# Two loads of q back in SyncE's queue, and the last output product split 384 to 128 columns

## The chip, the cores and the metric

The kernel runs on one core of one Trainium2 chip. The metric is the device time of the whole program in microseconds (us), of which several runs are taken; lower is better. A profiled execution gives the times inside: the span from the first to the last instruction, and the start and length of each instruction and DMA packet. A core has five engines that run side by side and meet at semaphores: TensorE (PE; its weight loads stand apart as PEld), VectorE (DVE), ScalarE (ACT), GpSimd (POOL) and SyncE (SP). DMAs are issued by SyncE, ScalarE or GpSimd, each in a queue of its own (q1, q10 and q0 in the profile), and all are carried by the same 16 DMA engines.

## The reference

A decaying linear attention over 4 batches, 8 heads, 768 tokens and 64 columns a head, in blocks of 64 tokens, and then a gated block with a product across tokens:

```python
for b in range(nb):                       # blocks of 64 tokens
    intra = einsum('bhic,bhjc->bhij', qb, kb) * Dmask
    intra = einsum('bhij,bhjd->bhid', intra, vb)
    inter = einsum('bhid,bhde->bhie', qb * lam_pow, kv_state)
    out[:, :, sl] = intra + inter
    kv_state = lam_block * kv_state + einsum('bhsd,bhse->bhde', kb * rev_pow, vb)
x = out.transpose(0, 2, 1, 3).reshape(B, S, 512)
h = maximum(x @ w_in, 0)                  # 512 -> 1024
u, v = h[..., :512], h[..., 512:]
v_n = (v - mean(v)) / sqrt(var(v) + 1e-6)
v_s = einsum('ts,bsd->btd', w_spatial, v_n) + b_spatial
result = (u * v_s) @ w_out                # 512 -> 512
```

Inputs and result are fp32.

## The kernel before

The 4 x 768 tokens are cut into 12 steps of 256 tokens, three to a batch (`n` from 0 to 11). A step loads 256 tokens of k, q and v for all heads, 512 KB each (`LK`, `LQ`, `LV`, in `load`, L191; three buffers for each input), casts them to bf16 (`KC`, `QC`; L174 to L178), multiplies v by powers of lam (`VD`, L314), turns k and q (by TensorE: `TK`, `TQ`, L328; from step 7 on by a DMA), computes scores (`SC`, L369) and masks them (`MK`, L373), adds to the state (`KV`, L385; copied out by `SS`), forms the attention output (`AV`, L406 and L415; copied out by `EX`), and multiplies by the two halves of w_in (`PV`, L438, and `PU`, L485). The v half is normalised (`BN`, `RA`, `RD`, `VN`). When a batch's three steps are done, its product across tokens (`PW`, L506), bias (`GB`, L511), gate (`GM`, L517) and output product (`PO`, L522, for each of 6 tiles of 128 tokens) follow, woven among the next steps; `EO` copies a tile's output from PSUM to SBUF and `ST` stores it (L545).

The order of all this is written by hand: `ORDER` is a list of tokens, each an operation, its arguments and, as the last letter, the engine that issues it (T, D, A, P, S for TensorE, VectorE, ScalarE, GpSimd, SyncE). `LQ.1.2.A` is the load of q of step 1, whole, issued by ScalarE; `LQ.1.2.S` the same by SyncE. Each engine takes its own tokens in the order of the list; tokens of other engines between them mean nothing to it. Waits between engines follow from the data and the buffers.

SyncE issues the loads in the order k0, k1, v0, v1, k2, q2, v2, q3, k3, ... ScalarE issues lam, then q0 and q1. GpSimd issues the weights: two halves of w_in (`WI`, L257), two of w_spatial (`WS`, L262), later w_out. It has these tokens in this order (casts and products of its own among them): k0's cast, `GT.0.1` (a one-element copy named "seen", L253, which waits until k of step 1 has landed), `WI.0`, q1's cast, `VD.1.0`, `WI.1`, `VD.1.1`, k2's cast, `WS.1`, `GT.2.1` (the same for v of step 1), `WS.0`, `VD.2.0`, `VD.2.1`. So the weights' transfers start when loads of k, v and k have come in and GpSimd has got that far.

TensorE begins with products on a constant tile (`WU`, L212), then takes q0 and k0, k1, the scores of step 0, the state, q1 and so on; `TQ.2.6` (q of step 2) comes after the first `PV`s, and `KV.2.0` after two `PU`s.

The last tile of the last batch (`t` = 4) is done in two halves of 256 columns: `PH` (L528) multiplies a half, `EH` copies it out (the first by ScalarE, the second by VectorE), `SH` stores it (the first in ScalarE's queue, the second in SyncE's; L541).

Of the kernel before, what the change touches and what calls it, by code (L numbers as in the profile page):

```python
# [13 lines left out]


ORDER = """
LK.0.2.S lam.A LQ.0.2.A LQ.1.2.A pos.P LK.1.2.S LV.0.2.S idn.P WU.-8.T LB.1.T msk.P LN.1.A LL.D LX.A KC.0.2.P
LT.0.A LV.1.2.S QC.0.2.D mkc.A WU.29.T TQ.0.6.T LK.2.2.S TK.0.1.T GT.0.1.P WI.0.P KC.1.2.D EK.0.1.A EQ.0.6.D
WU.5.T TK.1.4.T LQ.2.2.S LT.1.A SC.0.1.5.T SC.0.0.1.T VD.0.0.D VD.0.1.D LV.2.2.S LT.2.A MK.0.0.1.D WU.7.T
KV.0.0.T QC.1.2.P MK.0.1.5.D EK.1.4.A WU.8.T TQ.1.2.T LQ.3.2.S SS.0.0.A AV.0.0.0.T EQ.1.2.D VD.1.0.P SY.0.0.A  # L20
# [63 lines left out]
def kernel(  # L84
# [13 lines left out]
    P = 128  # L98
    B, H, S, D = q.shape
    DM = H * D  # L100
# [68 lines left out]
    def bank(b, n=1):  # L169
        return ps[:, b] if n == 1 else ps[:, b:b + n]  # L170

    def copy(e, o, i):
        if e == "A":
            nc.scalar.activation(out=o, in_=i, func=AF.Copy)  # L174
        elif e == "D":
            nc.vector.tensor_copy(out=o, in_=i)  # L176
        else:
            nc.gpsimd.tensor_copy(out=o, in_=i)  # L178
# [344 lines left out]
                             rhs=wout_sb[:, f, :], start=(f == 0), stop=(f == NCH - 1))  # L523

    def p_h(e, bb, t, b, x):
        half = slice(x * (DM // 2), (x + 1) * (DM // 2))
        for f in range(NCH):
            nc.tensor.matmul(out=bank(b)[:, half], lhsT=gT[bb % 2][:, f, t * P:(t + 1) * P],  # L528
                             rhs=wout_sb[:, f, half], start=(f == 0), stop=(f == NCH - 1))
# [2 lines left out]
        copy(e, o_sb[:, (bb * NT + t) % NO], bank(b))  # L532

    def e_h(e, bb, t, b, x):
        half = slice(x * (DM // 2), (x + 1) * (DM // 2))
        copy(e, o_sb[:, (bb * NT + t) % NO, half], bank(b)[:, half])

    def s_h(e, bb, t, x):
        half = slice(x * (DM // 2), (x + 1) * (DM // 2))
        eng = {"S": nc.sync, "A": nc.scalar}[e]  # L540
        eng.dma_start(out=out[bb, t * P:(t + 1) * P, half], in_=o_sb[:, (bb * NT + t) % NO, half])  # L541

    def st_o(e, bb, t):
# [4 lines left out]
               LK=ld_k, LQ=ld_q, LV=ld_v, KC=k_c, QM=q_m, DK=d_k, DQ=d_q, QC=q_c, VD=v_d, TK=t_k, TQ=t_q, EK=e_k, EQ=e_q,  # L548
               SC=s_c, MK=m_k, KV=k_v, SS=s_s, AV=a_v, SY=s_y, EX=e_x, PV=p_v, EV=e_v, BN=b_n, RA=r_a, RD=r_d,
               VN=v_n, PU=p_u, EU=e_u, WT=w_t, EW=e_w, PW=p_w, GB=g_b, GM=g_m, PO=p_o, EO=e_o, ST=st_o, EH=e_h, SH=s_h, PH=p_h)  # L550
    with tc.manual_schedule():
        for token in ORDER.split():
# [32 lines left out]
```

## Time and profile before

| | |
|---|---|
| time, median of 3 runs | 156.41 us (155.68 to 156.83) |
| the profiled execution's own time | 155.68 us |
| its span | 154.0 us |
| mean granted TensorE clock | 0.989 |
| TensorE busy | 137.1 us (89%) |
| VectorE, ScalarE, GpSimd busy | 106.1, 89.9, 69.8 us |
| SyncE's queue q1 | 27.01 MB, 68.6% of 16 engines' span |
| GpSimd's queue q0 | 2.75 MB, 10.3% |
| ScalarE's queue q10 | 1.18 MB, 3.0% |
| loads of q by ScalarE, of k by SyncE | 8.1 and 7.1 us from issue to landing (median) |

A share is a mean over stages that have different limits. The chain that ended last is followed back from the last instruction: at each step to what released it. It goes through TensorE for 68% of the span, DVE 10%, waits for DMAs 9%, SyncE's issues 6%. A wait is put down to the releaser that came last by the profile; where that one shares no data with the waiting instruction, it was another. Times below are counted from the span's start.

### The profile page before, as it was taken

To read this page: it belongs to the slowest core of one execution; us is meant where nothing else is said; L and a number is where in the kernel's file an instruction comes from. 1 tells how busy PE (TensorE), PEld (TensorE's weight loads), DVE (VectorE), ACT (ScalarE), POOL (GpSimd) and SP (SyncE) were. 2 spreads that over 40 slices of the span, in tenths; PEclk is the share of its full clock that TensorE was granted. 3 is DMA by queue.
4 is the path that set the end of the run, shared out by engine and by line. 5 is a ranking of instruction groups with operands and counts; after the bars stand their busy time and mean duration, and the time that the engine had idled before them with its cause. 6 is when DMAs were issued, how large, how long until landed. Compare 5 with 4: busy or idle time off the path is not lost.

```text
span 154.0 us, 4860 instructions
## 1 busy us (share of the span) xinstructions
PE 137.1 (89%) x2060; PEld 90.5 (59%) x2075; DVE 106.1 (69%) x191; ACT 89.9 (58%) x167; POOL 69.8 (45%) x83
## 2 busy tenths in 40 slices
PE   6967774969999999839999999999999999999990
PEld 4746542456876786635565657655676756565540
DVE  1247724688999679989976778885469888748300
ACT  3968373566850677417799824678373647960270
POOL 7435650055008999827255564564644002014700
PEclk9999998799999999999999999999999999999999
DMA  3999999999999969965999997999797000052364
GB/s 91 300 290 289 237 241 235 220 281 257 281 285 285 257 169 280 235 165 105 231 282 172 245 233 184 320 201 288 164 292 172 2 6 0 0 198 79 136 231 178
DMA packets 54152, 31.25 MB, mean 203 GB/s; under 512 B 11634, under 2 KB 51058, under 8 KB 54130
## 3 DMA queue, kind: packets, MB, share of 16 engines
q1 hardware_dynamic: 49520, 27.01, 68.6%
q0 software_dynamic: 2384, 2.75, 10.3%
q10 hardware_dynamic: 2226, 1.18, 3.0%
q8 instruction: 16, 0.26, 0.7%
q14 instruction: 6, 0.05, 0.1%
HBM read 24.77 MB, written 6.29 MB: 202 GB/s over the span
## 4 chain that ended last, share of the span: by engine, by line
PE 68%; DVE 10%; DMA 9%; SPq 6%; ACT 2%; issue 2%; POOL 1%; DVEq 0%
PE ps L506 19%; PE ps L522 13%; PE ps L438 11%; PE ps L485 10%; DMA q_in<-in_q_dram 9%; SPq L191 6%; DVE gT L517 3%; PE ps L369 3%; PE ps L415 3%; DVE a_sb L373 2%; PE ps L328 2%; PE ps L385 2%; PE ps L406 2%; PE ps L498 1%; POOL vd L314 1%
## 5 line engine op out<-in xcount | busy, mean ns | idle before, releaser
L517 POOL TENSOR_TENSOR gT<-vsb,uT 128x384 bf16<-128x384 f32 x24 | 21.8, 917 | 40.1 <-DVE vsb L511 31.4
L506 PE MATMUL ps<-wt_sb,vn 128*128 128x384 bf16 x192 | 33.9, 326 | 0.0
L373 DVE TENSOR_TENSOR a_sb<-ps,m 128x1024 bf16<-128x1024 f32 x24 | 28.6, 1216 | 2.2 <-PE ps L369 1.9
L314 POOL TENSOR_TENSOR vd<-v_in,lv 128x512 bf16<-128x512 f32 x19 | 19.6, 1043 | 18.5 <-DVE a_sb L373 10.7
L506 PEld LDWEIGHTS <-vn 128*128 128x128 bf16 x192 | 18.3, 98 | 11.9
L485 PE MATMUL ps<-xT,win_sb 128*128 128x256 bf16 x192 | 24.4, 273 | 0.0
L438 PE MATMUL ps<-win_sb,xT 128*128 128x512 bf16 x87 | 23.6, 400 | 0.4
L511 DVE TENSOR_TENSOR vsb<-ps,bsp 128x384 f32<-128x384 f32 x32 | 17.2, 550 | 9.5 <-PE ps L506 9.5
L522 PE MATMUL ps<-wout_sb,gT 128*128 128x512 bf16 x86 | 21.4, 379 | 0.4 <-issue 0.2
L443 ACT ACTIVATE vh<-ps 128x512 bf16<-128x512 f32 x23 | 13.7, 596 | 13.4 <-PE ps L438 12.4
L485 PEld LDWEIGHTS <-win_sb 128*128 128x128 bf16 x192 | 18.4, 98 | 4.9
L174 ACT ACTIVATE o_sb<-ps 128x512 f32<-128x512 f32 (+1 forms) x23 | 13.1, 586 | 11.3 <-PE ps L522 11.3
L174 ACT ACTIVATE xT<-ps 128x512 bf16<-128x512 f32 x22 | 15.2, 742 | 6.6 <-PE ps L415 6.4
L453 DVE BATCH_NORM_STATS2 st<-vh 128x6 f32<-128x512 bf16 x24 | 16.3, 679 | 2.7 <-ACT vh L443 2.6
L438 PEld LDWEIGHTS <-xT 128*128 128x128 bf16 x96 | 9.2, 102 | 10.4 <-issue 1.7
L385 PE MATMUL ps<-vd,kc 64*64 64x64 bf16 x320 | 8.9, 193 | 6.2 <-DVE s_sb L176 2.9
L522 PEld LDWEIGHTS <-gT 128*128 128x128 bf16 x92 | 8.8, 98 | 9.3 <-issue 0.2
L443 ACT ACTIVATE uT<-ps 128x512 bf16<-128x512 f32 x20 | 11.7, 596 | 2.8 <-PE ps L485 2.4
L299 POOL TENSOR_TENSOR qc<-q_in,lqn 128x512 bf16<-128x512 f32 x10 | 10.7, 1071 | 5.1 <-DMA q_in<-in_q_dram 4.7
L385 PEld LDWEIGHTS <-kc 64*64 64x64 bf16 x320 | 7.4, 109 | 8.3 <-issue 7.3
L174 ACT ACTIVATE s_sb<-ps 128x256 bf16<-128x256 f32 x16 | 6.1, 382 | 8.3 <-PE ps L385 7.4
L415 PE MATMUL ps<-a_sb,vd 64*64 64x128 bf16 x384 | 10.5, 217 | 0.3 <-DVE a_sb L373 0.3
(72 smaller groups left out, 179.7 us busy)
## 6 DMA issues: line engine op xcount, KB each, us to landing
k_in<-in_k_dram SPq DMA_DIRECT2D x12, 512.0 KB, 7.1
v_in<-in_v_dram SPq DMA_DIRECT2D x12, 512.0 KB, 6.9
out_dram<-o_sb SPq DMA_DIRECT2D x23, 256.0 KB, 3.1
q_in<-in_q_dram SPq DMA_DIRECT2D x10, 512.0 KB, 7.8
wsp_raw<-in_moe_w_spatial_dram POOLq DMA_DIRECT2D x2, 576.0 KB, 11.0
q_in<-in_q_dram ACTq DMA_DIRECT2D x2, 512.0 KB, 8.1
win_sb<-in_moe_w_in_dram POOLq DMA_DIRECT2D x2, 512.0 KB, 9.7
wout_sb<-in_moe_w_out_dram POOLq DMA_DIRECT2D x1, 512.0 KB, 9.3
```

Source lines behind the costliest of these rows:

```text
L174: nc.scalar.activation(out=o, in_=i, func=AF.Copy)
L314: vec(e).tensor_tensor(out=vd[n % NCA].rearrange("p (o i w) m d -> p o i (w m) d", o=2, i=2)[o], in0=v_in[n % NIN].rearrange("p (o i w) m ...
L373: nc.vector.tensor_tensor(out=a_sb[n % NA][:, i].rearrange("p o w j x -> p (o w) (j x)"), in0=bank(b, 2).rearrange("p o (w y) -> p (o w) y ...
L385: nc.tensor.matmul(out=pkv[row(o), u], lhsT=kc[n % NCA][row(c), u, m, o, :], rhs=vd[n % NCA][row(c), 4 * o + u, m, :], start=new and u == ...
L438: nc.tensor.matmul(out=bank(b), lhsT=x[:, g % 2, c, c ^ (g // 2)], rhs=win_sb[:, g, DH:DFF], start=(g == 0), stop=(g == NCH - 1))
L443: nc.scalar.activation(out=o, in_=i, func=AF.Relu)
L453: nc.vector.bn_stats(out=st6[p2][:, t], in_=vh[p2][:, t])
L485: nc.tensor.matmul(out=pu[:, f2].rearrange("p (c x) -> p c x", c=2), lhsT=win_sb[:, g, f * P:(f + 1) * P], rhs=x[:, 4 * i + o:4 * i + 4 - ...
L506: nc.tensor.matmul(out=bank(b)[:, 0:HW], lhsT=vn[bb % 2][:, s, f * P:(f + 1) * P], rhs=wt_sb[:, s, i * HW:(i + 1) * HW], start=(s == 0), s ...
L511: nc.vector.tensor_tensor(out=vsb[(bb * 4 + f) % NVS][:, i * HW:(i + 1) * HW], in0=bank(b)[:, 0:HW], in1=bsp[:, i * HW:(i + 1) * HW], op=A ...
L517: vec(e).tensor_tensor(out=gT[bb % 2][:, f, cols], in0=vsb[(bb * 4 + f) % NVS][:, cols], in1=uT[bb % 2][:, f, cols], op=ALU.mult)
L522: nc.tensor.matmul(out=bank(b), lhsT=gT[bb % 2][:, f, t * P:(t + 1) * P], rhs=wout_sb[:, f, :], start=(f == 0), stop=(f == NCH - 1))
```

## The change

It has two parts. The loads of q of steps 0 and 1 are issued by SyncE and no longer by ScalarE: that of step 0 after k of step 0, that of step 1 after v of step 0, so that SyncE's queue has k0, q0, k1, v0, q1, v1, k2, q2, v2, ... And the two parts of the last tile's output product, of its copies and of its stores are 384 and 128 columns wide in place of 256 and 256. Nothing else differs.

```diff
 ORDER = """
-LK.0.2.S lam.A LQ.0.2.A LQ.1.2.A pos.P LK.1.2.S LV.0.2.S idn.P WU.-8.T LB.1.T msk.P LN.1.A LL.D LX.A KC.0.2.P
+LK.0.2.S lam.A pos.P LQ.0.2.S LK.1.2.S LV.0.2.S idn.P WU.-8.T LB.1.T msk.P LN.1.A LL.D LQ.1.2.S LX.A KC.0.2.P
 LT.0.A LV.1.2.S QC.0.2.D mkc.A WU.29.T TQ.0.6.T LK.2.2.S TK.0.1.T GT.0.1.P WI.0.P KC.1.2.D EK.0.1.A EQ.0.6.D
...
     def p_h(e, bb, t, b, x):
-        half = slice(x * (DM // 2), (x + 1) * (DM // 2))
+        half = (slice(0, 3 * P), slice(3 * P, DM))[x]
...
     def e_h(e, bb, t, b, x):
-        half = slice(x * (DM // 2), (x + 1) * (DM // 2))
+        half = (slice(0, 3 * P), slice(3 * P, DM))[x]
...
     def s_h(e, bb, t, x):
-        half = slice(x * (DM // 2), (x + 1) * (DM // 2))
+        half = (slice(0, 3 * P), slice(3 * P, DM))[x]
```

## Prediction

> **What bounds the kernel now.** I read the page's slices first, then the chain that ended last, the timeline around its stalls, and the DMA views. The first row below is TensorE's busy share in 40 slices of 3.85 us, the second its granted clock.
>
> ```profile
> PE   6967774969999999839999999999999999999990
> ...
> PEclk9999998799999999999999999999999999999999
> ```
>
> From slice 18 (69 us) on TensorE is full, so an early shift of the chain passes to the end nearly whole. The time that can move lies ahead of 35 us, and in the last microseconds. There the chain (start, length, what) reads:
>
> ```profile
> 10.24 14.16 DMA q_in<-in_q_dram
> ...
> 24.49 0.70 DVE qc L176
> ...
> 25.25 0.82 PE ps L328 x8
> ...
> 32.04 2.03 POOL vd L314 x2
> ...
> 34.11 0.25 PE ps L385 x5
> ```
>
> Two loads set it: q of step 2, and (behind "POOL vd") v of step 2. The timeline, with the idle time before each group in brackets:
>
> ```profile
> 10.13 0.70 POOL L253 COPY seen<-k_in 1x1 f32<-1x1 f32 x1 [3.79 <-DMA k_in<-in_k_dram]
> ...
> 10.78 0.92 POOL L257 DMA_DIRECT2D win_sb<-in_moe_w_in_dram  x1
> ...
> 25.25 0.82 PE L328 MATMUL ps<-ident,qc 128*128 128x128 bf16 x8 [2.49 <-DVE qc L176]
> ...
> 32.02 2.04 POOL L314 TENSOR_TENSOR vd<-v_in,lv 128x512 bf16<-128x512 f32 x2 [10.73 <-DVE a_sb L373]
> ...
> 33.10 0.31 PE L385 MATMUL ps<-vd,kc 64*64 64x64 bf16 x8 [0.55 <-POOL vd L314]
> ...
> 34.11 0.25 PE L385 MATMUL ps<-vd,kc 64*64 64x64 bf16 x5 [0.69 <-POOL vd L314]
> ```
>
> Each load raises its semaphore sixteen times, once per DMA engine, and the trace keeps these times. Last ones: k0 5.25, q0 7.54, k1 10.08, q1 11.91, v0 12.48, v1 14.26, k2 16.02. Of q2, fifteen engines have landed at 20.27 and one at 24.40; of v2, fourteen at 24.61, one at 25.98, one at 31.87. GpSimd's vd of step 2 starts 0.15 after that 31.87, the lag that the other loads show on GpSimd; the page's releaser, a DVE mask that ended in the same instant, shares no data with it. So single late engines set both stalls. Why late: GpSimd's three bursts of weights (the halves of w_in from 14.9 and 20.0, w_spatial from 24.1 to 31.5) share the engines with SyncE's queue packet for packet (here 21.0 to 21.5 us: queue, packets, MB, share):
>
> ```profile
> q0 software_dynamic: 70, 0.07, 84.0%
> q1 hardware_dynamic: 70, 0.04, 35.0%
> ```
>
> and one engine loses 1.18 us more to a 16 KB instruction packet at 15.21. It has half of q2's 64 packets left when burst two begins, then much of v2's when burst three begins. The loads' rate in and between bursts, and the halved clock after the 2.49 us gap (columns: stretch, length, five engines' busy time, granted clock, DMA share, GB/s):
>
> ```profile
> 14.00:15.00 1.00, 0.79 (x13) 0.70 (x13) 1.00 (x2) 0.67 (x1) 0.60 (x1) 1.00 1.16 290
> ...
> 16.00:17.00 1.00, 0.71 (x19) 0.48 (x16) 1.00 (x2) 0.16 (x1) 0.98 (x2) 1.00 1.20 206
> ...
> 26.00:28.00 2.00, 2.00 (x7) 0.62 (x6) 1.47 (x3) 0.20 (x1) 0.00 (x0) 0.50 1.15 217
> ```
>
> **The change, part by part.** *Issues.* ScalarE loses two DMA issues (0.44 and 0.59 us). Its first table load can start 1.1 earlier, but the logarithm after it waits for TensorE's broadcast of lam (3.08 to 3.67) anyway: 0. If that cover were gone, 1.1 at most. SyncE gains both: q0 goes ahead of k1, v0 and all later loads, q1 between v0 and v1. An issue costs about 0.5 where the queue has room; from the fourth load on SyncE stands waiting for room in any case (3.54 to 20.19 nearly without a break). No new semaphore wait arises.
>
> *Order of landing.* 0.524 MB at 290 GB/s is 1.81 us per load, and the six loads up to v1 fill the time from k0 to v1 at this rate: 5.25 + 5 x 1.81 = 14.30 against 14.26 seen. In one queue I therefore get q0 7.06, k1 8.87, v0 10.68, q1 12.49, v1 14.30, and k2 at 16.11 if nothing cuts in. k1 and v0 gain 1.2 and 1.8, q1 loses 0.6. The first masks and step 1's scores come some 1.2 to 1.8 earlier; alone this is worth 0, because q2's wait covers it.
>
> The Trainium skill (DMA: Bandwidth & Descriptors, Issuing engines are not separate DMA queues) says that issuing on several engines saves sequencer time only, as all transfers interleave on the same engines. The trace agrees on the rate: 290 GB/s with both queues in turn (8 to 10 us) and with SyncE's alone (12 to 14). By that rule the head would be worth 0 and the sum 156.4; I don't follow it to there.
>
> *What hangs on k1.* GpSimd's "seen" waits for k1 and lets w_in go: issue 0.70 after the landing, first packets 4.1 after the issue (10.78 to 14.9). Now 8.87 + 0.70 + 4.1 = 13.7. A load's packets end some 0.9 before it lands: v1's at 13.4, so it slips through; k2, which before was done as the burst began, is caught. In 15 to 18 us the burst let 346 packets of SyncE's queue through where 3 us otherwise carry 1720, so it costs 2.4: k2 lands at 18.5, and 1.2 later, 19.7, on the engine that the instruction packet hits. GpSimd casts k2 at 18.61 before, held until then by TensorE's last use of that buffer (18.06 to 18.47), which now comes 1.2 to 1.8 sooner. So the cast starts between 18.6 and 19.8, and w_spatial behind it on GpSimd (issued 19.59) goes out 0 to 1.2 later; I take 1.1, since an instruction fetch ahead of 17 us is likely. Its user, the transposes at 40.17, has 7.0 us of slack. Burst two hangs on v1 (14.30) and stays near 20.0; q2 on its late engine stays near 24.4 (bounds 21.5 and 26.1, see the rivals).
>
> *What v2 gains.* Burst three starts at 25.2 instead of 24.1. On the late engine some 44 packets of v2 go at 0.15 us each in that burst (53 in 0.5 us over sixteen engines); in a burst-free microsecond at 290 GB/s an engine moves 35. So v2 lands near 26 to 27, vd is ready before TensorE asks, and the stall goes. It is worth: 34.42, where step 2's state product is through, minus 32.56, where the product before it ended, minus 0.3 of its own work, 1.5; the two bracketed waits alone give 1.24. Next in line is the DVE mask of step 2 (ends 32.02), just in time, and k3 (35.41), needed by TensorE at 42.31 only. I take -1.5; bounds 0 and -1.9.
>
> *Clock.* TensorE's gap before q2 grows from 2.5 to some 4 us, as the work before it is earlier. The row halves the clock for 3.41 us (25.52 to 28.93), about 1.7 lost; bounds of a change 0 and +0.8, taken +0.2. [...]
>
> *The end.* Four matmuls of 384 and four of 128 columns stream as many columns as eight of 256 (0.89): 0. ScalarE's copy grows from 0.38 (256 columns) toward 0.60 (512), so 0.49, and starts 0.2 later, about 149.85: its store goes out at 150.37, not 150.11. DVE's shrinks by 128/0.96 ns from 0.43 to 0.30: SyncE's store goes at 150.40, not 150.53. The stores land 2.1 after issue (152.26 and 152.62 before); ScalarE's now carries 192 KB and takes up to 0.2 more, so 152.5 to 152.7. Taken 0, bounds -0.15 and +0.2.
>
> Sum: -1.5 + 0.2 + 0 = -1.3. The profiled execution ran 155.68 (span 154.0 and 1.7 around it), the lowest of three; it would become 154.4. Against the median 156.41: **155.1**, faster by 0.8%, just inside the 1% that a measurement of this kernel can tell from no change. Chance 0.42; its own range 154.2 to 156.1.
>
> **Rivals.** *Nothing moves* (0.20): burst three doesn't wait, because the fetch misses k2's engine, and v2's last engine stays at 31.9. For it: two tails, both in the bursts. Time 156.4.
>
> *q2 falls behind burst two* (0.25, slower): SyncE's queue carried only 16 packets from 4.5 to 5.5, between k0 and k1, which ScalarE's queue filled with 560. If that hole belongs to the queue, it stands open now and all loads come up to 1.0 later, while the slow engine has 43 instead of 32 packets of q2 left at burst two; 11 are then left for burst three at 0.15 us each. Price 1.7, or 2.7 with the hole; it decides when more than 32 are left and the third burst follows within 0.3 us. Against it: later boundaries of SyncE's loads (v0 to v1, v1 to k2) show no hole. Time 158.1.
>
> *q2 comes free too* (0.13): if v1 is caught by burst one, GpSimd's vd of step 1 and so burst two go out later, and q2 lands near 21.5 on all engines. Then 2.0 more of q2's stall goes, until the second w_in half, due about 26, holds the next product. Against it: v1's margin of 0.3. Time 156.4 - 1.5 - 2.0 = 152.9.
>
> **From cases to numbers.** Below 154.85 lie nearly all of the last rival and under half of the forecast: faster 0.32. Within 1% the rest of the forecast and most of *nothing moves*: 0.40. Slower 0.28: the second rival and the unlucky ends of the others. The range 153.1 to 158.2 reaches from the good rival to the slow one.
>
> **What would show it.** Right: win_sb issued near 9.6 in place of 10.78, w_spatial near 20.7, k2 landing after 18, vd of step 2 starting before 29, no wait of TensorE at L385 near 33, the end chain as long as before. Wrong: k1 landing after 10 (the hole), q2 landing after 25, or vd of step 2 still starting near 32.

## The result, and the profile after

The changed kernel took 148.87 us (median of 4 runs, 147.07 to 149.44) against 156.62 for the kernel before (4 runs, 155.68 to 157.28): a ratio of 0.947, 95% interval 0.937 to 0.958, so 5% faster. I had predicted 155.1 and a range down to 153.1. The profiled executions took 149.44 us (span 147.7) after and 155.68 (span 154.0) before. The first is the longest of its four and the second the shortest, so the spans differ by 6.24 us where the medians differ by 7.75; the account below is of the 6.24.

The page of the kernel after, TensorE's busy tenths and granted clock in 40 slices (of 3.69 us here):

```profile
PE   6998674999999999999999999999999999999990
PEclk9999996899999999999999999999999999999998
```

Two things differ from the rows of before. The halved clock comes some 2 us earlier. And the row is full from slice 7 on, whereas the row of before has an 8 and a 3 in slices 16 and 17 (61.6 to 69.3 us). The prediction showed that row and read it as full "from slice 18 on", and asked nothing about the 3.

**The head did what was predicted, and more.** From the timeline of the kernel after (start, busy time, engine, line, what; in brackets the idle time before it and what ended it; lines of other instructions are left out at "..."):

```profile
9.49 0.92 POOL L257 DMA_DIRECT2D win_sb<-in_moe_w_in_dram  x1
...
24.14 1.04 PE L328 MATMUL ps<-ident,qc 128*128 128x128 bf16 x8 [2.79 <-DVE qc L176]
...
25.75 2.04 POOL L314 TENSOR_TENSOR vd<-v_in,lv 128x512 bf16<-128x512 f32 x2 [3.43 <-DMA v_in<-in_v_dram]
...
30.99 0.38 PE L385 MATMUL ps<-vd,kc 64*64 64x64 bf16 x12
```

GpSimd asks for w_in at 9.49 (10.78 before). q of step 2 reaches TensorE at 24.14 (25.25). GpSimd's product with v of step 2 starts at 25.75 (32.02), and the state product at 30.99 waits for nobody, where before it waited twice (0.55 and 0.69). The first long product across tokens (L506) starts at 41.83, before at 44.82: 3.0 us gained.

**Another 2.8 us came from a place that the prediction never looked at.** From the timeline of the kernel before:

```profile
59.89 1.04 POOL L299 TENSOR_TENSOR qc<-q_in,lqn 128x512 bf16<-128x512 f32 x1
...
60.05 5.15 DVE L517 TENSOR_TENSOR gT<-vsb,uT 128x384 bf16<-128x384 f32 x1
...
60.89 1.03 POOL L314 TENSOR_TENSOR vd<-v_in,lv 128x512 bf16<-128x512 f32 x1
...
61.89 1.03 POOL L299 TENSOR_TENSOR qc<-q_in,lqn 128x512 bf16<-128x512 f32 x1
...
62.89 1.03 POOL L314 TENSOR_TENSOR vd<-v_in,lv 128x512 bf16<-128x512 f32 x1
...
63.89 0.90 POOL L517 TENSOR_TENSOR gT<-vsb,uT 128x384 bf16<-128x384 f32 x1
...
67.78 0.44 PE L385 MATMUL ps<-vd,kc 64*64 64x64 bf16 x16 [2.92 <-DVE s_sb L176]
```

VectorE's gate product (`GM.0.3.0.D`, L517) takes 0.55 where nothing disturbs it. Here it takes 5.15, beside five GpSimd products that follow each other without a gap. VectorE's next copies (normalisation statistics, the state `s_sb`) queue behind it, and TensorE stands idle for 2.92 us. The same place after:

```profile
56.89 1.04 POOL L299 TENSOR_TENSOR qc<-q_in,lqn 128x512 bf16<-128x512 f32 x1
...
57.52 0.83 DVE L517 TENSOR_TENSOR gT<-vsb,uT 128x384 bf16<-128x384 f32 x1
...
57.89 1.36 POOL L314 TENSOR_TENSOR vd<-v_in,lv 128x512 bf16<-128x512 f32 x1
```

The product got in behind the first GpSimd product, and it was GpSimd that waited (1.36 in place of 1.04). In the windows from 65 to 70 us TensorE was busy for 2.12 of 5 us before and for 5.00 after. Behind this place the kernel after is 5.82 us ahead, and it stays so, matmul by matmul, up to the last output product.

**The end** gave the last 0.41. From the timeline after:

```profile
144.25 0.29 DVE L176 COPY o_sb<-ps 128x128 f32<-128x128 f32 x1 [4.63 <-PE ps L528]
144.55 0.40 ACTq L541 DMA_DIRECT2D out_dram<-o_sb  x1
144.57 0.33 SPq L541 DMA_DIRECT2D out_dram<-o_sb  x1
```

From the start of VectorE's last copy to the end of the span it is 3.48 us after and 3.89 before. In sum 2.99 + 2.84 + 0.41 = 6.24, the difference of the spans.

One thing must be known to read the times below: the executions of the kernel before fall into two groups, over all runs 9 of 55 at 148.5 to 151.2 us and 46 at 153.5 to 159.4, while all 10 of the kernel after lay at 146.7 to 149.5; "lower" and "upper group" mean this. All four of the kernel before in the result above are of the upper group; from the median of its lower group (149.37) to the median of the ten after (148.22) it is 1.15 us. So most of the 5% is that the upper group is gone.

### The profile page after: what moved, and what is told of

It is laid out like the page before. It is cut to its first block, busy times and chain, and to the rows that moved or that the text cites. A ratio compares the mean times of both kernels' runs of the same rounds, so it can differ in the third digit from the quotient of the medians.

```text
span 147.7 us, 4859 instructions
## 1 busy us (share of the span) xinstructions
PE 136.9 (93%) x2060; PEld 90.5 (61%) x2075; DVE 100.8 (68%) x191; ACT 89.8 (61%) x167; POOL 70.5 (48%) x83
## 4 chain that ended last, share of the span: by engine, by line
PE 78%; DMA 9%; SPq 6%; ACT 2%; DVE 1%; issue 1%; DVEq 0%
PE ps L506 21%; PE ps L438 14%; PE ps L522 13%; PE ps L485 13%; DMA q_in<-in_q_dram 9%; SPq L191 6%; PE ps L369 4%; PE ps L415 3%; PE ps L328 3%; PE ps L385 3%; PE ps L406 2%; PE ps L498 1%; ACT xT L174 1%; ACT vh L443 1%; PE ps L528 1%
## 5 line engine op out<-in xcount | busy, mean ns | idle before, releaser
L517 POOL TENSOR_TENSOR gT<-vsb,uT 128x384 bf16<-128x384 f32 x24 | 21.8, 918 | 37.1 <-DVE vsb L511 28.3
L506 PE MATMUL ps<-wt_sb,vn 128*128 128x384 bf16 x192 | 33.9, 326 | 0.0
L506 PEld LDWEIGHTS <-vn 128*128 128x128 bf16 x192 | 18.2, 98 | 11.9
L314 POOL TENSOR_TENSOR vd<-v_in,lv 128x512 bf16<-128x512 f32 x19 | 19.9, 1061 | 10.3 <-DMA v_in<-in_v_dram 6.6
L485 PE MATMUL ps<-xT,win_sb 128*128 128x256 bf16 x192 | 24.4, 273 | 0.0
L438 PE MATMUL ps<-win_sb,xT 128*128 128x512 bf16 x87 | 23.0, 392 | 0.5
L299 POOL TENSOR_TENSOR qc<-q_in,lqn 128x512 bf16<-128x512 f32 x10 | 10.7, 1073 | 5.9 <-DMA q_in<-in_q_dram 5.5
L178 POOL CAST kc<-k_in 128x1024 bf16<-128x1024 f32 x6 | 6.5, 1084 | 10.8 <-DMA k_in<-in_k_dram 10.1
L212 PE MATMUL ps<-warm 128*128 128x256 bf16 x61 | 9.8, 322 | 1.5 <-DVE warm L210 1.3
L174 ACT ACTIVATE kT<-ps 128x1024 bf16<-128x1024 bf16 x6 | 6.1, 1022 | 7.7 <-PE ps L328 7.2
```

Source lines behind the costliest of these rows:

```text
L314: vec(e).tensor_tensor(out=vd[n % NCA].rearrange("p (o i w) m d -> p o i (w m) d", o=2, i=2)[o], in0=v_in[n % NIN].rearrange("p (o i w) m ...
L438: nc.tensor.matmul(out=bank(b), lhsT=x[:, g % 2, c, c ^ (g // 2)], rhs=win_sb[:, g, DH:DFF], start=(g == 0), stop=(g == NCH - 1))
L485: nc.tensor.matmul(out=pu[:, f2].rearrange("p (c x) -> p c x", c=2), lhsT=win_sb[:, g, f * P:(f + 1) * P], rhs=x[:, 4 * i + o:4 * i + 4 - ...
L506: nc.tensor.matmul(out=bank(b)[:, 0:HW], lhsT=vn[bb % 2][:, s, f * P:(f + 1) * P], rhs=wt_sb[:, s, i * HW:(i + 1) * HW], start=(s == 0), s ...
L517: vec(e).tensor_tensor(out=gT[bb % 2][:, f, cols], in0=vsb[(bb * 4 + f) % NVS][:, cols], in1=uT[bb % 2][:, f, cols], op=ALU.mult)
```

## The experiments

My theory after the two profiles: the head lets the chain come 3 us earlier, so the gate product of step 0 of head group 3 reaches VectorE before GpSimd's run has got going, and its wait of 4 to 5 us goes; that wait, and not the head's 3 us, makes the two groups of times. The rival: the head or the tail give the whole gain directly, and the long product is a by-product.

### Each half of the change alone

The head alone (`ORDER` as after, halves of 256 columns), and the tail alone (`ORDER` as before, 384 and 128 columns):

> The loads of q of steps 0 and 1 in SyncE's queue, the last product in equal halves as before. Theory (loads): of the 6.3 us between the two profiled spans 3.0 come before 35 us from earlier landings of q2 and v2, 2.9 between 58 and 67 us from a DVE gate product that takes 0.8 in place of 5.2, and 0.4 at the end; so the span here is 148.0 to 148.2 and the time some 5.9 under the kernel before. Rival (tail): the split is worth more than it looks and the time stays within 2 us of the kernel before.

> The kernel before with only the 384 to 128 split. Theory: SyncE's last store lands first and its walk through eight final waits (0.06 each) runs while ScalarE's store is still under way, so the span shrinks by 0.4 (0.3 to 0.6) to about 153.6, nothing else moves. Rival (the prediction's term): 0, from -0.15 to +0.2.

The head alone took 147.24 to 150.01 in six executions and 154.32 to 164.8 in four; the profiled span was 146.9 us, below the 148.0 to 148.2 that I had expected. The tail alone took 148.31 (the profiled one), 156.03, 156.39 and 158.47. So the head goes most of the way, but the tail seemed to have a part in how often the lower group is met, and I ran both again.

> The head of the change alone, output halves equal, run again. Theory: the change of the tail does nothing to the product's wait at 58 us; this kernel's executions spread as those of the kernel after, at least five of six at 147 to 150.5 us, and its median is 0 to 1 us above. Rival: the tail has a part in it; half of the executions or more lie at 153 to 158 us.

> The tail of the change alone, loads of q as before, run again. Theory: it spreads as the kernel before, with four of six executions or more at 154 to 158.5 us. Rival: the tail has a part in it; half of the executions or more lie at 147 to 151 us.

The head alone: 11 of 13 at 146.98 to 150.33, two at 154.79 and 156.0; together 17 of 23 in the lower group. The tail alone: one of six there (150.29), the rest at 155.51 to 157.21; together 2 of 10, as the kernel before with 9 of 55. The head carries the change. The 10 of 10 of the whole change against 17 of 23 is too few to call the tail's part in it shown or refuted.

What the upper group is, shows in the profiles. One profile of the head alone fell in each group. In the lower one (148.58), from its timeline:

```profile
56.00 0.55 DVE L517 TENSOR_TENSOR gT<-vsb,uT 128x384 bf16<-128x384 f32 x1
56.55 1.04 POOL L299 TENSOR_TENSOR qc<-q_in,lqn 128x512 bf16<-128x512 f32 x1 [0.55 <-DMA q_in<-in_q_dram]
```

GpSimd stood waiting for q of step 7 to land, and the product ran in that gap without any wait. In the upper one (156.0) the clock was halved from 19.07 to 29.30 in place of 3.4 us, the chain came late, the product reached VectorE at 59.38, 0.41 into GpSimd's run from 58.97, and took 4.92.

### The product itself, moved off VectorE

```diff
-KC.6.2.A GM.0.3.0.D PV.4.1.0.T
+KC.6.2.A GM.0.3.0.P PV.4.1.0.T
```

in the kernel before (first text) and in the kernel after (second):

> The kernel before, with the gate product GM.0.3.0 on GpSimd in place of VectorE. Theory (port): the 5.2 us of that product are a wait for GpSimd's run of products, and TensorE's 2.9 us of idle at 64.9 hang on it; without it the span falls by 2.5 to 3 us, to about 151.3, and vd and q of the next steps come at most 0.9 later on GpSimd, which has cover. Rival (handed on): the stall only hides another wait, for the loads or for GpSimd, and the span stays within 1 us of 154.0.

> The kernel after, with the gate product of head group 3, step 0 (line 517) done by GpSimd in place of VectorE. Theory: what the change wins beyond its 3 us at the head is that this product no longer waits 4 to 5 us for GpSimd's run; with the product on GpSimd itself there is nothing to wait for, so all executions lie together, at 147 to 149.5 us, and none near 155. Rival: the wait is not the cause of the two groups of times; then the product's 1 us on GpSimd only adds to GpSimd's run and some executions still lie at 154 to 158 us.

In the kernel before this one token gave 149.87, 151.3, 151.79 and 152.54: no execution near 156, with the loads of q where they were, though three of the four lie a little above the lower group. The profile shows v of step 2 as late as ever (30.63); set beside the kernel before matmul by matmul, TensorE was 0.15 us behind at 59 us, 2.84 ahead at 67.78, behind the product, and 3.13 ahead from 72 us on. The edit moves nothing else. In the kernel after: 146.78 to 149.65 (5 runs, median 149.48), all together. It does not beat the kernel after, which no longer waits there.

### The chain made late again

24 idle matmuls in TensorE's stream of the kernel after, with the product on VectorE (first) and on GpSimd (second):

```diff
-SC.3.0.0.T VD.3.0.D SC.3.1.3.T
+WU.24.T SC.3.0.0.T VD.3.0.D SC.3.1.3.T
```

> The kernel after, with 24 idle matmuls of 128x256 (by the rows of the warm-up, some 0.11 to 0.13 us each, 2.6 to 3.1 us in all) put into TensorE's stream at about 39 us, so that the chain is as late at 58 us as it was in the kernel before. Theory: the gate product on VectorE then comes again into GpSimd's run, waits its 4 to 5 us, and the time rises by more than the idle matmuls, by 5 to 6 us, to 153 to 157 us. Rival 1: the delay is passed on as it is, 150.5 to 152 us. Rival 2: the slack behind takes it, 148 to 149.5 us.

> The kernel after with both edits: the 24 idle matmuls at 39 us, and the gate product of step 0 of head group 3 on GpSimd. Theory: with no VectorE product to wait for GpSimd's run, the delay is passed on as it is and no more: 150 to 152 us, 3 to 5 us below the one with the delay alone. Rival: the time of the late chain does not hang on this product, and it lies with the one with the delay alone, within 1 us.

The idle matmuls took 2.6 us. With the product on VectorE: 154.06 to 155.58 in four executions and 149.87 in one (median 154.84), 6.0 to 7.5 above the two medians of the kernel after (148.87, and 147.32 further below). With the product on GpSimd: 149.67 to 151.6 (median 149.81). So with the same idle matmuls it takes 5 us more where the product must wait. From the timeline of the first:

```profile
57.84 1.04 POOL L299 TENSOR_TENSOR qc<-q_in,lqn 128x512 bf16<-128x512 f32 x1
...
58.56 4.61 DVE L517 TENSOR_TENSOR gT<-vsb,uT 128x384 bf16<-128x384 f32 x1
...
65.74 0.44 PE L385 MATMUL ps<-vd,kc 64*64 64x64 bf16 x16 [2.37 <-DVE s_sb L176]
```

The delay brought the wait back, and TensorE's idle time with it. But the wait is not all of the 5 us. The granted clock in 40 slices, from the pages of the first and of the second:

```profile
PEclk9999959999999999987999999999999999999999
```

```profile
PEclk9999999999999999999999999999999999999999
```

Matmul by matmul, the first is 0.65 us behind the second ahead of the product, 3.44 behind it at 67.6 us, and 4.99 from 71 us on. So 2.8 are the wait, and 1.55 a stretch of halved clock from 67.50 to 70.91 that follows it (slices 17 and 18) and that the second doesn't have. Five of the nine profiles with the long wait have such a stretch between 66 and 74 us; none of the eight without it has one between 38 and 145 us. That the idle time of TensorE brings it on is likely, but no run took the two apart.

The size of the delay itself came out at 0.3 between the medians of the two kernels with the product on GpSimd (149.81 and 149.48). The profiled executions tell more: the one with the idle matmuls is 0.47 behind ahead of them, 3.09 behind them and 3.02 at the end. There the 2.6 is passed on whole, as expected.

### What makes the loads of step 2 early

Both loads of w_spatial of the kernel after asked for earlier, so that their burst stands in front of v of step 2:

```diff
-KV.0.1.T EX.0.0.0.A VD.1.1.P MK.1.1.2.D
+KV.0.1.T EX.0.0.0.A VD.1.1.P WS.1.P WS.0.P MK.1.1.2.D
```

(and taken away behind `KC.2.2.P` and `GT.2.1.P`).

> The kernel after, with both loads of w_spatial asked for by GpSimd earlier, behind its last product with v of step 1 (some 17 us) and so before the copy of k of step 2, in place of 19.5 to 20.6 us. Theory: the weights' third burst then stands in front of v of step 2, which lands at 29 to 32 us in place of 25.6; the first state product of step 2 waits again, the chain is 1.5 to 3 us later at 58 us, the gate product waits for GpSimd's run, and the time is 152 to 157 us. Rival: what makes the head faster is the loads of q alone, which stay as they are; the time stays within 1 us of the one after, at 148 to 150 us.

155.28 to 158.63 (5 runs, median 157.27): the whole gain gone, with the loads of q as in the kernel after. The timeline:

```profile
31.59 2.04 POOL L314 TENSOR_TENSOR vd<-v_in,lv 128x512 bf16<-128x512 f32 x2 [10.85 <-DMA v_in<-in_v_dram]
32.68 0.42 PE L385 MATMUL ps<-vd,kc 64*64 64x64 bf16 x8 [3.06 <-POOL vd L314]
```

The middle one of v's sixteen engines had landed at 25.27, the last at 31.45: the lone late engine of the kernel before again, made by the order of a burst alone. At the end of that wait the clock was halved, from 32.45 to 39.27, which adds to the loss. Further down the product came at 63.08 and took 4.21.

The opposite in the kernel before, both loads of w_spatial behind `VD.2.1.P`:

> The kernel before, with both loads of w_spatial issued behind the vd products of step 2 in place of ahead of them. Theory (bursts): v2's last engine lands near 25 in place of 31.9, vd of step 2 starts near 25 and the two waits at L385 (0.55 and 0.69) go; q2 stays at 24.4. The chain at 34 us is 1.5 to 1.9 earlier (1.24 at the least), the span 152.1 to 152.8, unless the gate product's stall near 60 changes with it. Rival (engine): v2's last engine is slow for another reason than the burst, lands after 29, and the span stays at 154.0.

v of step 2 landed at 25.85, as the theory has it, and the chain was 3.7 us ahead at 34 us. But the time rose to 159.35 to 160.62. The profile says why:

```profile
41.18 4.05 PE L498 MATMUL ps<-ident,wsp_raw 128*64 128x128 bf16 x72 [4.62 <-DMA wsp_raw<-in_moe_w_spatial_dram]
```

The second half of w_spatial landed at 41.13 and TensorE waited 4.62 for it; the chain was late, and the product, at 64.41, took 4.51. The mechanism of v was right, but my edit used up the slack of w_spatial.

Which of the two loads of q counts (only one token moved in the kernel before):

> The kernel before, with only the load of q of step 1 moved to SyncE, behind v of step 0; q of step 0 stays on ScalarE. Theory: what counts at the head is that q of step 1 no longer shares the DMA engines ahead of k of step 1, so that k of step 1 lands at 8.6 to 9 us in place of 9.9 to 10.1, GpSimd asks for the first half of w_in at 9.3 to 9.6 us in place of 10.6 to 10.8, all bursts behind it come over a us earlier for the loads of step 2, and v of step 2 lands at 25 to 27 us: as the full head change, 146 to 151 us in most executions. Rival: both loads are needed; then v of step 2 lands at 27 to 32 us and most executions lie at 154 to 158 us.

> The kernel before, with only the load of q of step 0 moved to SyncE, between k of step 0 and k of step 1; q of step 1 stays on ScalarE. Theory: q of step 1 still shares the engines ahead of k of step 1, which lands at 9.8 to 10.1 us, the first half of w_in is asked for at 10.5 to 10.8 us, and everything is as before: v of step 2 at 27 to 32 us, most executions at 154 to 158 us. Rival: it is q of step 0 whose move counts; k of step 1 lands near 8.7 us and most executions lie at 146 to 151 us.

With q of step 1 moved, k of step 1 landed at 8.77, w_in was asked for at 9.47 and v of step 2 landed at 25.73: the landings of the full change. With q of step 0 moved, k of step 1 landed at 10.51, w_in was asked for at 11.21 and v of step 2 landed at 29.82: near those before. So the landings hang on q of step 1, as expected. The times do not follow as cleanly: three of five executions in the lower group for each (147.94 to 148.86, and 147.49 to 148.65). For q of step 0 that is a miss: I expected most of them near 156. A kernel with late landings can still be lucky later, as the tail alone was at 148.31, when v landed at 27.38; five executions don't tell how often.

### How the kernel after spreads, and a filled gap

> The kernel after, unchanged, run again, to see how its executions spread. Theory: with the chain 3 us earlier the gate product comes at the start of GpSimd's run or before it in most executions, so at least two thirds lie at 147 to 150.5 us and the rest at 153 to 157 us. Rival: a spread like that of the kernel before, most of them at 154 to 158 us.

146.75 to 149.21 (6 runs, median 147.32). In its profile the product ran at 54.87 for 0.55, before GpSimd's run from 56.06.

In the kernel after with the product on GpSimd, `WU.20.T` ahead of `TQ.2.6.T`:

> The kernel after with the gate product of step 0 of head group 3 on GpSimd and 20 idle matmuls of 128x256 (some 2.3 us at full clock) on TensorE ahead of the transposes of q of step 2, in the gap of 1.6 to 2.8 us in which TensorE waits for them. Theory: TensorE's granted clock is then not halved behind that gap; the 1 us that the halved clock costs in some executions is gone, the idle matmuls may reach 0.5 us past the end of the gap, and the time is 146.5 to 148.5 us, all executions together. Rival: the clock is halved whether the gap is filled or not, or the fill reaches past the gap by more: 148.5 to 150.5 us.

147.78 to 149.87 (median 148.99), four of five in the rival's range: nothing gained. The clock was halved from 20.65 to 24.06; that began 2.1 us ahead of the first idle matmul (22.75), so the idle matmuls took 2.99 us and not 2.3. They reached past the gap: VectorE's cast of q of step 2 was done at 23.95, and TensorE came to its transposes at 25.58. So the rival was right by its second half, and whether a filled gap keeps the clock up isn't shown by this run. No version here beats the kernel after.

### What the product waits for

One more DMA asked for by GpSimd in the kernel before, in the middle of the run (`d_g` reads a third of w_spatial into a tile that nothing uses):

```diff
-BN.4.1.D VD.6.1.P PU.4.0.4.T
+BN.4.1.D DG.P VD.6.1.P PU.4.0.4.T
```

> The kernel before, with one more DMA asked for by GpSimd right behind its first product of the run that VectorE's gate product waits for (a third of w_spatial, read once more into a tile of its own that nothing uses; its asking takes GpSimd some 0.8 us in which it works on no tile). Theory: the gate product waits because GpSimd's products follow each other without a gap; it gets in at this gap, takes at most 2.3 us in place of 4 to 5.2, and the time falls by 2.5 to 4 us, to 151 to 154.5 us. Rival: the product waits for something else that ends with the whole run (its own data, or the last product of the run); it takes 5 to 6 us, and the time stays at 155 to 158.5 us.

Four of five executions took 156.01 to 157.82, the rival's time, and one 152.84; the profiled one is at 156.3 (the median). From its timeline:

```profile
60.57 1.03 POOL L303 TENSOR_TENSOR qc<-q_in,lqn 128x512 bf16<-128x512 f32 x1
...
61.48 4.36 DVE L521 TENSOR_TENSOR gT<-vsb,uT 128x384 bf16<-128x384 f32 x1
61.55 0.80 POOL L267 DMA_DIRECT2D gap_sb<-in_moe_w_spatial_dram  x1
...
62.37 1.06 POOL L318 TENSOR_TENSOR vd<-v_in,lv 128x512 bf16<-128x512 f32 x1
...
63.38 1.04 POOL L303 TENSOR_TENSOR qc<-q_in,lqn 128x512 bf16<-128x512 f32 x1
...
64.38 1.04 POOL L318 TENSOR_TENSOR vd<-v_in,lv 128x512 bf16<-128x512 f32 x1
...
65.38 1.23 POOL L521 TENSOR_TENSOR gT<-vsb,uT 128x384 bf16<-128x384 f32 x1
```

(The lines are four further down here: L521 is the gate product, L318 and L303 are L314 and L299.) The product did not get in while GpSimd asked for the DMA (61.6 to 62.37); my theory of what counts as a gap falls. It took 4.36, between the theory's 2.3 and the rival's 5 to 6, and ended at 65.84, before the run's end, and GpSimd's last product, 1.23 in place of 0.9, waited for it. So the rival's reason, an end of the whole run, is not right either.

All profiles with the product on VectorE side by side (us):

| kernel | run of GpSimd begins | product begins | takes | time of the execution |
|---|---|---|---|---|
| after again | 56.06 | 54.87 | 0.55 | 146.75 |
| tail alone | 56.53 | 55.43 | 0.55 | 148.31 |
| head alone | 56.55 | 56.00 | 0.55 | 148.58 |
| after | 56.89 | 57.52 | 0.83 | 149.44 |
| only q of step 1 moved | 57.45 | 58.35 | 4.43 | 154.76 |
| after, 24 idle matmuls | 57.84 | 58.56 | 4.61 | 154.84 |
| only q of step 0 moved | 58.59 | 58.88 | 5.04 | 155.48 |
| head alone, again | 58.97 | 59.38 | 4.92 | 156.0 |
| before | 59.89 | 60.05 | 5.15 | 155.68 |
| before, DMA in the run | 60.57 | 61.48 | 4.36 | 156.3 |
| tail alone, again | 61.01 | 62.05 | 4.28 | 156.39 |
| after, w_spatial early | 61.97 | 63.08 | 4.21 | 158.63 |
| before, w_spatial late | 63.59 | 64.41 | 4.51 | 159.35 |

All four executions without the long wait are in the lower group, all nine with it in the upper. A product that is reached at 57.5 us or earlier is through at once or nearly so (0.83 in the kernel after), one that is reached at 58.3 or later waits. Three of the four were reached before GpSimd's run began. The fourth, the profiled execution of the kernel after itself, was not: it came 0.63 us into the run, while products that came between 0.16 and 1.11 us into it waited in the other nine. So the time of arrival sorts these thirteen, but why that one got in is not shown, and in that execution the 2.8 us may be luck, though all ten executions of the kernel after are in the lower group.

## Why the prediction was wrong

**The step that failed is the first one**: "From slice 18 (69 us) on TensorE is full, so an early shift of the chain passes to the end nearly whole. The time that can move lies ahead of 35 us, and in the last microseconds." The first of these sentences held for what reaches 69 us: the 5.82 us that the kernel after is ahead at 70 us are 5.82 at the end. The second put the wait at 58 to 65 us at nothing, and it was worth nearly half the gain, 2.84 of 6.24. The chain that ended last in the kernel before had it in one row:

```profile
58.92 1.22 DVE a_sb L373
60.14 5.07 DVE gT L517
65.21 0.61 DVE st L453
```

A product of 128x384 that takes 5 us on the path, where its kin take 0.55 (its group of eight: median 0.58, longest 5.15), is a wait in disguise: no bracket marks it on VectorE's row, since VectorE counts as busy. Its trace on TensorE did have a bracket, the 2.92 us behind `s_sb` shown above, longer than either wait at L385 that I priced; the prediction leaves it among what does not move, and so misses what `s_sb` had waited for. An early shift is not passed on as it is where two engines' orders meet by time: in these two executions 3 us of shift came with 2.84 more.

**The head, term by term.** Landings were right to 0.1 for the loads up to v of step 1 (predicted 7.06, 8.87, 10.68, 12.49, 14.30 for q0, k1, v0, q1, v1; seen 6.98, 8.79, 10.60, 12.40, 14.21), w_in at 9.49 (9.6), k of step 2 at 19.49 (18.5 to 19.7), w_spatial at 20.61 (20.7), v of step 2 at 25.60 (26 to 27). The -1.5 for v of step 2 was right: both waits at L385 are gone. Set side by side matmul by matmul, it is 1.5. Two terms beside it were missed. q of step 2, taken as unmoved at 24.4, landed at 23.30, and TensorE got to its transposes 1.1 earlier; the case "q2 comes free too" had priced 2.0 for a better one and given it 0.13. Why it landed earlier was not taken apart. And the clock, booked at +0.2 for a gap ahead of q of step 2 that grows to some 4 us (it grew from 2.49 to 2.79), gave 0.4 back: the halved stretch (23.40 to 26.81, before 25.52 to 28.93) fell more on the idle time ahead of q of step 2. So -3.0 in place of -1.3.

**The tail**, booked at 0 with bounds of -0.15 and +0.2, gave -0.41, outside both. This term is well measured: from the start of VectorE's last copy to the end of the span it is 3.87 to 3.89 in the eight profiles with equal halves and 3.45 to 3.49 in the nine with 384 and 128 columns. The last landing is as late as before (2.56 us behind that copy's start, before 2.54), as I had worked out; but I stopped at the landing. Before, SyncE's store lands last, at 152.62, and SyncE then passes its final semaphore waits one by one until 153.13. After, SyncE's own store lands at 146.32, ScalarE's at 146.81, and SyncE is through its waits at 146.89. That the split of the tail does this is shown by those profiles, the tail alone among them (3.47); that it does so because SyncE's waits moved under ScalarE's transfer is read from the two traces.

**The rivals.** *Nothing moves* and *q2 falls behind burst two* did not come: no hole stood between k0 and q0, and q of step 2 was earlier, not later.

That a late chain puts the executions of the kernel after into the upper group is shown by the runs with w_spatial moved (5 of 5) and with the idle matmuls (4 of 5), and that the loads of q are what brings them out of it by the head alone (17 of 23 in the lower group, the kernel before 9 of 55). That there is no upper group without the wait of the gate product is shown by the four kernels with this product on GpSimd (19 of 19 executions at 146.8 to 152.5). The wait is not the whole distance between the groups: the medians of the two groups of the kernel before are 7.25 us apart (156.62 and 149.37), and with the product moved its median, 151.54, is still 2.2 above the lower one. What makes a single execution of the kernel before lucky (9 of 55) was not settled; the late engine of v of step 2 (27.38 in the lucky profile of the tail alone, 31.87 in that of the kernel before) and the length of the halved clock both vary from execution to execution.

## What to carry to other kernels

Look along the chain for instructions that take several times their group's median, and treat the excess as a wait, even if the profile calls the engine busy. Before costing a shift of a few microseconds, list the places where an instruction of one engine meets a run of another by time alone, and ask on which side of the run it falls after the shift: there a shift is not passed on, but multiplied or swallowed. A product that sits on the boundary can be moved to the engine whose run it would wait for; in the kernel before that was one letter in `ORDER`, and none of its four executions was in the upper group.

## What the runs showed of the hardware

VectorE's gate product, with both inputs in SBUF, waits while GpSimd works. In all nine cases the wait ends in the same way: the product ends 0.41 to 0.43 after the end of one GpSimd product, in eight of them the last of the run, and GpSimd's products in between run at their usual 1.03. The Trainium skill (SBUF — State Buffer, Who interferes with whom) says that a VectorE instruction with two SBUF inputs contends with a GpSimd instruction that reads SBUF. The same section calls the port pair that the two engines share an exclusive lock, and says that issue order decides who blocks. The runs agree that the product is blocked. They show a wait longer than one instruction: 3.7 to 4.6 us behind a GpSimd product of 1.04, and no entry in the 0.8 us in which GpSimd asked for a DMA. In the kernel after, the product got in at the end of the first GpSimd product, reached 0.63 into it; reached 0.72 into the same product (with idle matmuls), or 0.16 into it (before), it did not. What decides this was not settled.

The granted clock is halved in stretches of 3.41 us. Ahead of the last microseconds, three of the seventeen profiles have none (the tail alone at 148.31, the kernel after with the product on GpSimd at 146.78, the same with idle matmuls at 149.81), the others one to four, the first of them mostly somewhere between 18 and 37 us; in some they follow each other without a break (19.07 to 29.30 in the head alone at 156.0). A second one behind the gate product's wait, between 66 and 74 us, is what five of the nine profiles with that wait have.
